# A two-layer decode kernel: the loads around the layers' border, in contiguous quarters into rooms that come free by quarters

## The chip, the cores and the metric

The kernel runs on one core of one Trainium2 chip. The metric is the time of one execution in microseconds on the device; where several runs are shown, their median counts.

## The reference, cut to what matters

Four sequences decode one token each through two layers that share their weights and caches. Each layer is attention, then a feed-forward block:

```
x = x + attention(layernorm(x), k_cache, v_cache, wq, wo)
x = x + ffn(layernorm(x), w_gate, w_up, w_down)        # both lines twice
q = x @ wq                                             # 32 heads of 128, 4 to each of 8 key heads
o = softmax(q k^T / sqrt(128)) v  over 8192 keys;      out = o @ wo
ffn = (silu(x @ w_gate) * (x @ w_up)) @ w_down         # 512 -> 1792 -> 512
```

All tensors are bf16. One pair of a sequence and a key head, called a unit here, has 2 MB of keys and 2 MB of values (2.097 million bytes each); there are 32 units in a layer. The order of the 8192 keys of a unit makes no difference to the result, as long as keys and values are laid out in the same order.

## The kernel before, in words

**Rooms.** SBUF has eight rooms (slots 0 to 7 of `kvf`, line 200) of 2 MB: 128 partitions by 8192 elements, each in eight places of 1024 elements (`s{slot}.{q}`). A room takes the keys (K) or the values (V) of one unit. Slots 6 and 7 also take the feed-forward weights at the end of a layer (lines 202 to 212): the gate's from the start of slot 6 to the end of its place 6, a quarter of up's over the border of both slots, then down's in slot 7, in parts of 6, 6 and 2 of its 14 row blocks (`WD`, line 213). The other three quarters of up's weights have a room of their own.

**Order of the loads.** SP issues all transfers on one queue, in the order of the list `items` (lines 321 to 327). `pump` (line 373) issues the next ones as long as the room that `home` names (line 336) is free, and stops at the first whose room isn't. SP waits at each transfer until those who used the places are done. A whole unit is one transfer with rows of 32 KB (`runs`, line 345), wherever the rows fall. The last V of a layer (`split`, line 328) comes in four quarters of the free dimension, with rows of 4 KB.

**The border.** The second layer visits the units in the order 29, 30, 31, 0, 1, 2 and so on (line 310), because K and V of units 29 to 31 stay in slots 0 to 5 from the first layer (`kept`, line 320) and aren't loaded again. Below, K0 means the keys of unit 0 in the second layer, and so on. After the feed-forward weights the list goes on with K0, K1, V0, K2, V1, K3, V2, K4, V3, K5, V4, K6. K0 and K1 go to slots 6 and 7 once the last matmul with the down weights is done (`ffn`, lines 731 and 732). V0 takes K29's room and K2 takes K30's in two halves each (`halves`, line 330, and `half`, line 405), with rows of 8 KB, as the scores of the fourth and of the last of eight blocks are done (lines 538 to 541). V1, K3, V2 and V3 take the rooms of V29, K31, V30 and V31, K4 and K5 those of K0 and K1, V4 that of V0, K6 that of K2.

**Order of the work.** For a K, VectorE turns each block by a transpose of 32 x 32 (`turn`, line 451), and TensorE makes scores of it (`scores`, line 469, four matmuls a block); K29 to K31 are turned already. `keys` (line 527) writes down turning and scores block by block, the turning up to three blocks ahead. Then follow the maximum, the exponentials on ScalarE, and the transpose of the probabilities (`max_p` to `total`, lines 480 to 513), in steps of a list `line` that are put between the blocks after it. `values` (line 551) makes the weighted sums. A layer's list of work (`work`, line 312) is K29, K30, V29, K31, V30, K0, V31, K1, V0, K2, V1 and so on. The query projection is made for the first unit's heads at the start of a layer and for all others in one block (`qproj`, line 676): in the second layer in front of K0's scores (lines 807 and 808). GpSimd places a unit's query for its scores (`place_q`, line 459). TensorE's, VectorE's and ScalarE's instructions are recorded first and then played, the regular units as a loop (`roll`, line 740). In the second layer the loops begin with K2. All of them are issued from the helper lines 99 and 117, and the transfers from lines 133 and 135; so the profile has tiles rather than lines to go by.

Of the kernel before, what the change touches and what calls it, by code (L numbers as in the profile page):

```python
# [145 lines left out]
def bass_interleave_layers__gqa_block_cached__swiglu_ffn__decode_kernel(  # L146
# [44 lines left out]
    with ExitStack() as es:  # L191
# [75 lines left out]
        sem_h = [[sem(f"sem_h{k}{i}") for i in range(2)] for k in range(2)]  # L267
# [105 lines left out]
        def pump():  # L373
            while issued[0] < len(items):
# [19 lines left out]
                src = cache[b, g, :, :].rearrange("(p t) d -> p (t d)", p=P)  # L394
# [10 lines left out]
        def half(it, i):  # L405
            to = halves[it]
            kind, L, u = to
            s = slot_of[it]
            if i == 0:
                assert items[issued[0]] == to  # L410
                slot_of[to] = s
                issued[0] += 1
            w = SL // 2
            src = (A_k_cache if kind == "K" else A_v_cache)[u % B, u // B, :, :].rearrange("(p t) d -> p (t d)", p=P)
            T.dma("sp", [(kv[:, s, i * w:(i + 1) * w], src[:, i * w:(i + 1) * w])], sem_h[unit_order[1].index(it[2])][i],
                  writes=[f"s{s}.{i * NB // 2 + k}" for k in range(NB // 2)])

        def finished(it):
            kind, L, u = it
            if (kind, 1, u) in kept and L == 0:  # L420
                slot_of[kind, 1, u] = slot_of[it]
                if kind == "K":
                    turned.update((1, u, q) for q in range(NB))
            elif it in halves:
                half(it, 1)
                pump()
            else:
                free.add(slot_of[it])
                pump()
# [97 lines left out]
        def keys(L, u):  # L527
            def block(q):
# [9 lines left out]
                if q == NB // 2 - 1 and ("K", L, u) in halves:  # L538
                    half(("K", L, u), 0)
# [4 lines left out]

            for q in range(NB):
                if (L, u, q) not in turned:
                    turn(L, u, q)
                blocks.append((0.65, lambda q=q: block(q)))
                drain(LAG)
        done = set()  # L550
        def values(L, u):
# [36 lines left out]
            def add_rows():  # L588
                T.pe(bank(LNB)[:, 0:REP], acc[:], head[:], reads=["acc", "head"], writes=[f"pb{LNB}"],
                     start=True, stop=True)  # L590
                scale_o(LNB)
# [16 lines left out]
            def scale_o(k):  # L608
                T.op("dve", lambda e: e.tensor_tensor(oT[:, g // (G - 1), :, b], bank(k)[:, 0:REP], rl[:, rl_of[u], :],
# [66 lines left out]
        def qproj(gs, u=None):  # L676
            h0, nh = gs[0] * REP, len(gs) * REP
            for h in range(h0, h0 + nh):
                for kt in range(KT):
                    T.pe(bank(LNB)[:, h * B:(h + 1) * B], wq_sb[:, kt, h * Dh:(h + 1) * Dh], xn[:, kt * B:(kt + 1) * B],  # L680
                         start=(kt == 0), stop=(kt == KT - 1),
                         reads=[f"wq{kt}", "xn"], writes=[f"pb{LNB}"], sig=(kt == KT - 1))
            T.op("dve", lambda e: e.tensor_copy(qT[:, :, h0:h0 + nh],
# [15 lines left out]
        def ffn(last):  # L699
# [4 lines left out]
            rb = rstd[:].unsqueeze(1).to_broadcast([P, FO, B])  # L704
            for (w_sb, wname, bk) in (([wg_sb[:, k, :] for k in range(KT)], "wg", gb), (wu_sb, "wu", ub)):
                for fo in range(FO):
# [16 lines left out]
            for j, (a, b) in enumerate(WD):  # L723
                for nt in range(KT):
                    for fo in range(a, b):
                        T.pe(bank(dn[j])[:, nt * B:(nt + 1) * B], wd_sb[:, fo, nt * P:(nt + 1) * P],
                             hT[:, fo * B:(fo + 1) * B], start=(fo == a), stop=(fo == b - 1),
                             reads=["hT", f"wd{j}"] + at_w["wd"], writes=[f"pb{dn[j]}"], sig=(fo == b - 1))
                if j < len(WD) - 1:
                    add_to_x(dn[j])  # L730
            free.update((NKEEP, NKEEP + 1))
            pump()
# [65 lines left out]
        for L in range(2):  # L798
# [4 lines left out]
            qproj([first], unit_order[L][0])  # L803
            rest_q = [list(range(0, first)), list(range(first + 1, G))]
            assert (L, first) in ((0, 0), (1, G - 1))
            for i, (kind, _, u) in enumerate(work(L)):
                if L == 1 and (kind, u) == ("K", 0):
                    blocks.append((3.5, lambda gs=rest_q[0]: qproj(gs)))
                (keys if kind == "K" else values)(L, u)
                if L == 0 and i == 0:  # L810
                    drain(0.0)
                    qproj(rest_q[1])
# [45 lines left out]
```

## Time and profile before

| what | value |
|---|---|
| median of 3 runs | 650.14 us (649.64 to 650.25) |
| the profiled execution's own time | 651.29 us |
| its span, from the first to the last instruction | 649.3 us |
| TensorE (matmul) busy | 505.3 us, 78% |
| VectorE busy | 446.2 us, 69% |
| ScalarE busy | 116.3 us, 18% |
| moved by the transfers | 274.27 MB, a mean of 422 GB/s |
| mean granted TensorE clock | 0.855 |

The busy share of an engine is an average over the whole span. The kernel has a start, the first layer, a border of some 60 us around 350 us, the second layer, and an end, with different limits. So the views by stretches of time are of more use than the sums, above all those of the transfers: the rate in GB/s and the times of SP's issues.

### The profile page before, as it was taken

How to read it: one execution, taken by the hardware profiler on the slowest of the kernel's cores; microseconds unless marked ns; L12 is line 12 of the kernel's file. 1: busy time of each engine (PE TensorE's matmuls, PEld its weight loads, DVE VectorE, ACT ScalarE, POOL GpSimd, SP SyncE). 2: the span in 40 equal slices, each digit the busy share in tenths (PEclk: the TensorE clock that was granted, in tenths of full speed). 3: DMA queues.
4: the chain of work that ended last, by engine and by line, in shares of the span. 5: the costliest groups of instructions: out<-in, count | busy, mean ns of one | idle time of the engine just before them, and what ended most of it. 6: DMA issues, size and time to landing. Idle time of an engine off the chain costs nothing.

```text
span 649.3 us, 12407 instructions
## 1 busy us (share of the span) xinstructions
PE 505.3 (78%) x4896; PEld 324.7 (50%) x4896; DVE 446.2 (69%) x1079; ACT 116.3 (18%) x391; POOL 19.3 (3%) x73
## 2 busy tenths in 40 slices
PE   1657788878868787886877986898888787886886
PEld 1534454545435454553556654555555454553556
DVE  2556676776866767776762386979797777686683
ACT  0021111211211212221220211213131221121120
POOL 0000000000000000000000000000000000000000
PEclk9998787797987879789795978979897969799795
DMA  8999999999999999999999999999999999999996
GB/s 347 427 431 428 433 429 434 428 440 428 432 436 424 444 426 432 439 424 442 428 416 361 421 408 430 417 439 430 432 438 424 438 430 436 436 424 438 430 415 279
DMA packets 13085, 274.27 MB, mean 422 GB/s; under 512 B 2712, under 2 KB 2720, under 8 KB 3744
## 3 DMA queue, kind: packets, MB, share of 16 engines
q1 hardware_dynamic: 13056, 273.89, 98.7%
q8 instruction: 17, 0.28, 0.2%
q14 instruction: 12, 0.10, 0.0%
HBM read 273.88 MB, written 0.00 MB: 422 GB/s over the span
## 4 chain that ended last, share of the span: by engine, by line
DMA 50%; DVE 24%; PE 21%; issue 3%; SPq 1%; ACT 1%; DVEq 0%; POOL 0%; ACTq 0%; POOLq 0%
DMA kvf<-in_A_k_cache_dram 47%; PE ps L99 21%; DVE kvf L117 15%; DVE acc L117 4%; DMA kvf<-in_B_w_up_dram 3%; DVE one L117 1%; DVE pT L117 1%; SPq L135 1%; DVE m L117 1%; DVE scr L117 1%; ACT pb L117 0%; ACT acc L117 0%; DVE oT L117 0%; DVEq L782 0%; SPq L133 0%
## 5 line engine op out<-in xcount | busy, mean ns | idle before, releaser
L117 DVE STREAM_TRANSPOSE kvf<-kvf 128x512 f32<-128x512 f32 x488 | 322.3, 686 | 68.6 <-DMA kvf<-in_A_k_cache_dram 68.6
L99 PE MATMUL ps<-kvf,zq 128*128 128x256 bf16 x2048 | 332.6, 305 | 21.7 <-DVE kvf L117 16.4
L99 PEld LDWEIGHTS ps<-kvf,zq 128*128 128x128 bf16 x2048 | 202.6, 111 | 92.7 <-DVE kvf L117 40.2
L117 ACT ACTIVATE pb<-m 1x128 f32<-1x128 f32 x64 | 19.7, 308 | 441.1 <-DVE m L117 441.1
L99 PE MATMUL ps<-kvf,pT 128*16 128x512 bf16 x960 | 68.0, 407 | 1.4 <-DVE rl L117 1.4
L117 DVE SCALAR_TENSOR_TENSOR acc<-ps,own,acc 128x128 f32<-128x128 f32 x180 | 63.2, 351 | 6.5 <-ACT acc L117 1.9
L99 PE MATMUL ps<-identf,one 128*1 128x128 f32 x64 | 17.9, 279 | 43.2 <-DVE one L117 43.2
L117 DVE TENSOR_REDUCE one<-ps 128x1 f32<-128x256 f32 x64 | 25.9, 405 | 37.0 <-PE ps L99 36.5
L99 PEld LDWEIGHTS ps<-identf,one 128*1 128x1 f32 x64 | 5.1, 80 | 73.6 <-DVE one L117 67.5
L99 PE MATMUL ps<-head,acc 128*128 128x4 f32 x120 | 24.5, 275 | 21.4 <-DVE acc L117 21.3
L99 PEld LDWEIGHTS ps<-head,acc 128*128 128x128 f32 x120 | 20.5, 214 | 37.0 <-DVE acc L117 36.7
L117 ACT ACTIVATE pb<-ps,one,rstd 128x256 bf16<-128x256 f32 x64 | 36.1, 563 | 2.1
L467 POOL TENSOR_TENSOR zq<-scr,quad 128x64 bf16<-128x64 bf16 x62 | 18.1, 293 | 604.0 <-PE ps L99 564.9
L99 PEld LDWEIGHTS ps<-kvf,pT 128*16 128x16 bf16 x960 | 19.1, 91 | 33.8 <-issue 21.9
L99 PE MATMUL ps<-one,pb 1*128 1x1 f32 x128 | 26.2, 272 | 11.5 <-ACT pb L117 11.2
L99 PEld LDWEIGHTS ps<-one,pb 1*128 1x128 f32 x128 | 20.8, 202 | 28.8 <-ACT pb L117 26.0
L99 PE MATMUL ps<-o,wo_sb 128*128 128x4 bf16 x256 | 26.5, 166 | 9.1 <-DVE o L117 9.1
L117 DVE STREAM_TRANSPOSE pT<-pb 128x256 bf16<-128x256 bf16 x64 | 26.1, 408 | 9.7 <-ACT pb L117 9.7
L99 PEld LDWEIGHTS ps<-rsm,one 128*128 128x128 f32 x128 | 23.9, 232 | 12.2 <-ACT rsm L117 10.4
L99 PEld LDWEIGHTS ps<-o,wo_sb 128*128 (+1 forms) x256 | 22.8, 103 | 12.8 <-issue 9.0
L99 PE MATMUL ps<-rsm,one 128*128 128x4 f32 x128 | 21.7, 240 | 9.0 <-ACT rsm L117 9.0
L117 DVE TENSOR_TENSOR xT<-xT,ps 128x16 f32<-128x16 f32 x21 | 3.6, 172 | 33.1 <-PE ps L99 33.1
(61 smaller groups left out, 197.1 us busy)
## 6 DMA issues: line engine op xcount, KB each, us to landing
kvf<-in_A_k_cache_dram SPq DMA_DIRECT2D x60, 2048.0 KB, 28.8
kvf<-in_A_v_cache_dram SPq DMA_DIRECT2D x58, 2048.0 KB, 31.2
wq_sb<-in_A_wq_dram SPq DMA_DIRECT2D x4, 1024.0 KB, 8.4
wo_sb<-in_A_wo_dram SPq DMA_DIRECT2D x8, 512.0 KB, 37.7
kvf<-in_A_v_cache_dram SPq DMA_DIRECT2D x8, 512.0 KB, 14.7
kvf<-in_B_w_gate_dram SPq DMA_DIRECT2D x8, 448.0 KB, 16.8
kvf<-in_B_w_down_dram SPq DMA_DIRECT2D x14, 256.0 KB, 17.6
kvf<-in_B_w_up_dram SPq DMA_DIRECT2D x5, 448.0 KB, 18.0
```

The source lines that it names most:

```text
L99: return e.matmul(out, lhsT=lhsT if at is None else lhsT(place(at)), rhs=rhs, **kw)
L117: self.tape[engname].append((repr((name, args, kw)), lambda e, _: getattr(e, name)(*args, **kw), left, sig, None))
L135: ins = e.add_instruction(mybir.InstDMACopy(name=self.nc.get_next_instruction_name(), mode="Copy", queue="qSPDynamicHW", ins=e.lower_ap_dm ...
L467: T.op(eng, lambda e: e.tensor_tensor(dst, q4, m4_, ALU.mult), reads=keys_ + ["quad"], writes=["zq"])
```

## The change

The feed-forward weights' rooms are given up in pieces: three quarters of K0 are issued once the gate's matmuls are written down, the fourth after up's, half of K1 after the first part of down's, the other half at its end. For that, down's parts become 8, 4 and 2 row blocks, and each part waits for its own places alone. The rooms of K29 and K30 are given up by quarters, after every second block, not by halves. Each of these pieces is a contiguous quarter of the cache (2048 keys, 512 KB, rows of 16 KB). Units 0, 1 and 2 of the second layer and the last unit of both layers are loaded in such quarters, keys and values alike (`fours`), so that both have the same order. V31's values come ahead of K0's scores and behind the query projection, which is now split into seven blocks of matmuls (`qmul`) and one step behind them (`qrows`). V3 stands ahead of K4 in the list of loads. The blocks of K0 are turned among the scores of K30, those of K1 among K31's (`ahead`). The list of VectorE's instructions shows these 16 transposes at their new places; the loops begin with K2 as before, and TensorE has the same matmuls. The sum over rows in `add_rows` gets columns of its own in its bank.

```diff
+        WD = ((0, 8), (8, 12), (12, 14))
-                "wd": room(f1, f1 + FO * D)}
-        WD = ((0, 6), (6, 12), (12, 14))
+                **{f"wd{j}": room(f1 + a * D, f1 + b * D) + [f"wd{j}"] for j, (a, b) in enumerate(WD)}}
...
+        i, j = (items.index((k, 1, unit_order[1][2 * NRES + n])) for k, n in (("K", 1), ("V", 0)))
+        items[i], items[j] = items[j], items[i]
...
-        halves = {("K", 1, unit_order[1][k]): items[ends[0] + 3 + k] for k in range(2)}
+        heirs = {("K", 1, unit_order[1][k]): items[ends[0] + 3 + k] for k in range(2)}
+        fours = {(L, unit_order[L][-1]) for L in range(2)} | {(1, u) for u in unit_order[1][NRES:2 * NRES]}
...
                 if it in split:
-                    w = TT * Dh // NQ
-                    n8 = NB // NQ
+                    n = NB // NQ
                     for q in range(NQ):
-                        T.dma("sp", [(kv[:, s, q * w:(q + 1) * w], src[:, q * w:(q + 1) * w])], sem_l[q],
-                              writes=[f"s{s}.{q * n8 + k}" for k in range(n8)])
+                        part(it, s, q * n, (q + 1) * n, sem_l[q])
+                elif (L, u) in fours:
+                    part(it, s, 0, NB, sem_s[s])
...
+        def part(it, s, a, b, sem_):
+            kind, L, u = it
+            assert (L, u) in fours
+            n = NB // NQ
+            w, m = n * TB * Dh, S // NQ
+            src = (A_k_cache if kind == "K" else A_v_cache)[u % B, u // B, :, :]
+            T.dma("sp", [(kv[:, s, q * w:(q + 1) * w], runs(src[q * m:(q + 1) * m, :])) for q in range(a // n, b // n)],
+                  sem_, writes=[f"s{s}.{k}" for k in range(a, b)])
...
+        def quarter(it, i):
+            to = heirs[it]
             if i == 0:
+                place(to, slot_of[it])
+            n = NB // NQ
+            part(to, slot_of[it], i * n, (i + 1) * n, sem_h[unit_order[1].index(it[2])][i])
...
-                if q == NB // 2 - 1 and ("K", L, u) in halves:
-                    half(("K", L, u), 0)
+                if ("K", L, u) in heirs and (q + 1) % (NB // NQ) == 0 and q < NB - 1:
+                    quarter(("K", L, u), q // (NB // NQ))
...
+            i = unit_order[L].index(u)
+            ahead = unit_order[1][i + 2] if L == 1 and i in (1, 2) else u
             for q in range(NB):
-                if (L, u, q) not in turned:
-                    turn(L, u, q)
+                if (L, ahead, q) not in turned:
+                    turn(L, ahead, q)
...
+                if not last:
+                    if bk == gb:
+                        place(ks[0], NKEEP)
+                        part(ks[0], NKEEP, 0, w6, sem_p[0])
+                    else:
+                        part(ks[0], NKEEP, w6, NB, sem_p[1])
...
+                if j == 0 and not last:
+                    place(ks[1], NKEEP + 1)
+                    part(ks[1], NKEEP + 1, 0, NB // 2, sem_p[2])
+            if not last:
+                part(ks[1], NKEEP + 1, NB // 2, NB, sem_p[3])
...
+            if L == 1:
+                todo.remove(("V", 1, unit_order[1][2]))
+                todo.insert(todo.index(("K", 1, 0)), ("V", 1, unit_order[1][2]))
+            for i, (kind, _, u) in enumerate(todo):
+                if L == 1 and (kind, u) == ("V", unit_order[1][2]):
+                    for k in rest_q[0]:
+                        blocks.append((0.5, lambda k=k: qmul([k])))
+                    blocks.append((0.5, lambda gs=rest_q[0]: qrows(gs)))
```

More of the change, by code (lines that the diff above doesn't have):

```diff
@@ L266, in bass_interleave_layers__gqa_block_cached__swiglu_ffn__decode_kernel @@
         sem_l = [sem(f"sem_l{q}") for q in range(NQ)]
-        sem_h = [[sem(f"sem_h{k}{i}") for i in range(2)] for k in range(2)]
+        sem_h = [[sem(f"sem_h{k}{i}") for i in range(NQ)] for k in range(2)]
+        sem_p = [sem(f"sem_p{i}") for i in range(4)]
         sem_x = sem("sem_x")
@@ L403, in pump, with place @@
                 issued[0] += 1
[L405 to L408, printed above, removed]
-            if i == 0:
[L410 to L416, printed above, removed]
+        def part(it, s, a, b, sem_):
[6 more added lines that the diff above has]
+                  sem_, writes=[f"s{s}.{k}" for k in range(a, b)])
+        def place(it, s):
+            assert items[issued[0]] == it
+            slot_of[it] = s
+            issued[0] += 1
+        def quarter(it, i):
+            to = heirs[it]
+            if i == 0:
+                place(to, slot_of[it])
+            n = NB // NQ
+            part(to, slot_of[it], i * n, (i + 1) * n, sem_h[unit_order[1].index(it[2])][i])
         def finished(it):
@@ L423, in finished @@
                     turned.update((1, u, q) for q in range(NB))
-            elif it in halves:
-                half(it, 1)
+            elif it in heirs:
+                quarter(it, NQ - 1)
                 pump()
@@ L674, in deviation, with qmul @@
                  reads=["vs", bkey], writes=["rstd"])
-        def qproj(gs, u=None):
-            h0, nh = gs[0] * REP, len(gs) * REP
-            for h in range(h0, h0 + nh):
+        def qmul(gs):
+            for h in range(gs[0] * REP, (gs[-1] + 1) * REP):
                 for kt in range(KT):
@@ L802, in bass_interleave_layers__gqa_block_cached__swiglu_ffn__decode_kernel @@
             first = unit_order[L][0] // B
[L803 removed]
+            qmul([first])
+            qrows([first], unit_order[L][0])
             rest_q = [list(range(0, first)), list(range(first + 1, G))]
             assert (L, first) in ((0, 0), (1, G - 1))
[L806 to L808 removed]
+            todo = work(L)
+            if L == 1:
[6 more added lines that the diff above has]
+                    blocks.append((0.5, lambda gs=rest_q[0]: qrows(gs)))
                 (keys if kind == "K" else values)(L, u)
```

20 lines of the change are left out of this document (11 added, 9 removed).

## The prediction, made before the change was run

> **What bounds the kernel now.** I read the page's queues and its chain of waits first.
>
> ```profile
> q1 hardware_dynamic: 13056, 273.89, 98.7%
> ...
> DMA 50%; DVE 24%; PE 21%; issue 3%; SPq 1%; ACT 1%; DVEq 0%; POOL 0%; ACTq 0%; POOLq 0%
> ```
>
> The reader is to see that the transfers fill 98.7% of the span of 16 DMA engines, and that no other engine carries more than a quarter of the chain. So time is saved only where the transfers pause. Next, busy time by stretches; the last number of a row is GB/s, the one before it the busy share of the DMA engines, the third from the end the TensorE clock.
>
> ```profile
> 50.00:300.00 250.00, 198.79 (x1601) 122.43 (x1599) 178.12 (x418) 44.76 (x152) 7.61 (x26) 0.83 1.00 432
> 300.00:346.00 46.00, 36.18 (x500) 25.47 (x501) 29.46 (x79) 8.91 (x31) 0.88 (x3) 0.84 1.00 423
> 346.00:354.00 8.00, 4.74 (x111) 4.03 (x108) 2.05 (x12) 0.00 (x0) 0.00 (x0) 0.50 0.84 301
> 354.00:384.00 30.00, 27.68 (x316) 19.69 (x320) 12.58 (x33) 5.63 (x19) 1.17 (x4) 0.81 1.00 427
> 384.00:388.00 4.00, 3.35 (x35) 2.11 (x28) 3.92 (x10) 1.77 (x6) 0.00 (x0) 1.00 0.85 295
> ```
>
> The steady rate is 432 GB/s. Against it, 300 to 354 us loses 46 x (1 - 423/432) + 8 x (1 - 301/432) = 1.0 + 2.4 = 3.4 us, 354 to 384 loses 0.35, and 384 to 388 loses 4 x (1 - 295/432) = 1.3. Those 5.0 us are the ceiling of any gain at the border. Who feeds the queue there stands in the timeline of SP's issues (start, duration, count):
>
> ```profile
> 326.77 9.42 SPq L135 DMA_DIRECT2D kvf<-in_B_w_down_dram  x7
> 347.99 2.38 SPq L135 DMA_DIRECT2D kvf<-in_A_k_cache_dram  x2
> 356.84 3.07 SPq L133 DMA_DIRECT2D kvf<-in_A_v_cache_dram  x2
> 362.13 2.85 SPq L133 DMA_DIRECT2D kvf<-in_A_k_cache_dram  x2
> 365.63 0.48 SPq L135 DMA_DIRECT2D kvf<-in_A_v_cache_dram  x1
> 370.70 0.48 SPq L135 DMA_DIRECT2D kvf<-in_A_k_cache_dram  x1
> 371.69 0.47 SPq L135 DMA_DIRECT2D kvf<-in_A_v_cache_dram  x1
> 383.63 0.47 SPq L135 DMA_DIRECT2D kvf<-in_A_k_cache_dram  x1
> ...
> 390.67 0.47 SPq L135 DMA_DIRECT2D kvf<-in_A_k_cache_dram  x1
> ...
> 403.00 0.47 SPq L135 DMA_DIRECT2D kvf<-in_A_k_cache_dram  x1
> ```
>
> SP has nothing to issue from 336.2 to 347.99, and from 372.2 to 383.63: each time the queue runs dry behind it. The two transfers issued into the dry queue (347.99 and 383.63) show what that costs, in the issues by line with size and time to landing:
>
> ```profile
> kvf<-in_A_k_cache_dram SPq DMA_DIRECT2D x1, 2048.0 KB, 8.0
> kvf<-in_A_k_cache_dram SPq DMA_DIRECT2D x1, 2048.0 KB, 8.3
> ```
>
> A unit of 2.097 MB moves in 4.85 us at 432 GB/s, so an issue must come some 3.3 us before the queue is empty. My rule below: a transfer lands at the later of (the one ahead of it; its issue + 3.3), plus 4.85 us per unit or 1.21 per quarter. Tried on before, it gives K0 356.1, K1 361.0, V0 365.7, K2 370.6, V1 375.4, K3 380.3, V2 385.1, K4 383.63 + 3.3 + 4.85 = 391.8, and then V3 396.6, K5 401.5, V4 406.3.
>
> **Part 1, K0 and K1 in the feed-forward weights' rooms.** TensorE's timeline:
>
> ```profile
> 342.87 0.89 PE L99 MATMUL ps<-xn,kvf 128*128 128x4 bf16 x28
> 344.74 1.50 PE L99 MATMUL ps<-xn,kvf 128*128 128x4 bf16 x51 [0.98 <-DMA kvf<-in_B_w_up_dram]
> 347.62 0.29 PE L99 MATMUL ps<-xn,kvf 128*128 128x4 bf16 x5 [1.38 <-issue]
> 348.22 1.65 PE L99 MATMUL ps<-scr,kvf 128*128 128x4 bf16 x56 [0.31 <-DVE scr L117]
> ...
> 354.04 5.45 PE L99 MATMUL ps<-kvf,zq 128*128 128x256 bf16 x28
> ...
> 361.00 1.05 PE L99 MATMUL ps<-kvf,zq 128*128 128x256 bf16 x8
> ...
> 364.50 1.04 PE L99 MATMUL ps<-kvf,pT 128*16 128x512 bf16 x16
> ...
> 371.63 2.94 PE L99 MATMUL ps<-xn,wq_sb 128*128 128x4 bf16 x112
> ...
> 376.47 1.03 PE L99 MATMUL ps<-kvf,zq 128*128 128x256 bf16 x4 [0.83 <-POOL zq L467]
> ...
> 379.96 3.60 PE L99 MATMUL ps<-kvf,zq 128*128 128x256 bf16 x20
> ```
>
> The gate's matmuls end at 343.8, so three quarters of K0 are issued there; its last at 347.9 (up ends), K1's first half at 349.3 (32 of the 56 down matmuls), its second at 349.9. SP stands idle then and is not late; a quarter's issue takes it 0.33 to 0.5 us, as its rows show. Weights are issued by 336.2, ahead in the same queue, so they are not held up. With the weights landed by about 349.0, the rule gives K0 353.9 and K1 358.7: the queue does not run dry. The waits added at SP hold only transfers behind them that could not start earlier anyway.
>
> **Part 2, V0 and K2 by quarters.** K29's scores run from 352.9 to 359.5, 0.68 us per block (half way falls at the issue of 356.84), so V0's quarters are issued at 355.4, 356.8, 358.2 and 359.6 and land at 360.0, 361.3, 362.7, 364.1. K30's give K2's at 361.1, 362.1, 363.4, 364.65: landings 365.7, 366.9, 368.1, 369.3. V1 (V29's room, 365.6) lands at 374.1, K3 379.1, V2 383.9. Here the releases bind, and of the 2.4 us only 385.1 - 383.9 = 1.2 us is left.
>
> **Part 3, V31 ahead of K0, V3 ahead of K4.** V31's values move to just behind the query projection; V3 is issued at about 377.4, not behind K4. Needed by 383.9 - 3.3 = 380.6, it is in time: V3 lands at 388.8 where K4 landed at 391.8. The second pause (1.8 us by the rule) is gone; together 3.0 us at this point. K4 (K0's end, at the latest 384) is needed by 385.5, K5 by 390.3.
>
> **Part 4, K0 and K1 turned early.** VectorE's timeline:
>
> ```profile
> 359.54 0.42 DVE L117 TENSOR_REDUCE one<-ps 128x1 f32<-128x256 f32 x1 [6.53 <-PE ps L99]
> ...
> 376.99 2.48 DVE L117 STREAM_TRANSPOSE kvf<-kvf 128x512 f32<-128x512 f32 x4
> ```
>
> The same 16 transposes of 0.62 us go to where VectorE idled (6.5 us before K29's maximum). The first three stand ahead of that maximum in VectorE's order and wait for K0's landing: 353.9 + 1.9 = 355.8, before 359.5, so they hold nobody. Four more stand ahead of the transpose of K29's probabilities and delay it by up to 0.6 us, K30's by up to 0.5; V29 at 364.50 covers the first. Without cover: 0.5 us.
>
> What it buys is the compute chain that releases K6's room, and this decides how much of the 3.0 us stays. ScalarE's timeline:
>
> ```profile
> 46.95 0.26 ACT L117 ACTIVATE one<-ps,rstd 128x1 f32<-128x1 f32 x1 [6.47 <-issue]
> ...
> 398.42 0.26 ACT L117 ACTIVATE one<-ps,rstd 128x1 f32<-128x1 f32 x1 [5.40 <-issue]
> ```
>
> On entering its loop, in both layers, ScalarE stands for 5 to 6 us with nothing to wait for, and K2's last scores wait for its sums: hence K6 only at 403.0. After the change V4 lands at 403.3, so K6 must be issued by 400.0. The projection split in seven ends at about 375.5, V31 at 377.4, K0 starts then (376.5 before). Its 32 matmuls cost 0.18 us each (379.96's row, at half clock) or 0.13 (361.00's row). K0 ends at 384.0 if slow throughout, 382 if fast; K1, no longer bound by transposes, 4.9 later, at 388.9 or 387, against 390.6 (the issue at 390.67). The loop entry follows it: K6 at 401.2 or 399.3. Slow, the queue starves 401.2 + 3.3 - 403.3 = 1.2 us; fast, not at all. I take 0.5 (below), since both stretches of scores that began slow ended fast, after more than half of their time:
>
> ```profile
> 352.90:359.50 6.60, 6.57 (x34) 4.54 (x34) 0.11 (x1) 0.56 (x2) 0.00 (x0) 0.57 0.99 425
> 360.00:364.60 4.60, 4.60 (x41) 3.52 (x45) 0.91 (x3) 1.52 (x5) 0.00 (x0) 1.00 1.00 413
> 376.40:383.50 7.10, 6.79 (x40) 4.64 (x43) 5.87 (x13) 0.53 (x3) 0.01 (x1) 0.57 0.99 422
> ```
>
> The mean of 0.57 over 6.6 and 7.1 us is some 6 us at 0.5 and 1 us at 1.0; K0 follows V31, which starts the work at 376.4, so the last quarter of K0 should run fast: two thirds of the way from fast to slow, K6 at 400.5, 0.5 us. The Trainium skill (TensorE: Matmul & The Clock Gate, Part 1) states otherwise: some 3.4 us of sustained work double the clock. By that rule K0 would be fast from about 379.8, and the estimate would be no starving and -3.1 us in all; K29, busy 6.57 of 6.60 us at a mean of 0.57, speaks against it, and the trace goes into my sum.
>
> **Part 5, contiguous quarters.** In long runs:
>
> ```profile
> 330.00:332.50 2.50, 2.50 (x28) 1.76 (x31) 1.90 (x5) 1.21 (x4) 0.00 (x0) 1.00 1.00 411
> 361.00:369.00 8.00, 7.62 (x72) 5.27 (x70) 3.17 (x10) 3.29 (x11) 0.29 (x1) 1.00 1.01 421
> ```
>
> Rows of 4 KB go at 411, of 8 KB at 421, of 32 KB at 432; rows of 16 KB I put between the last two. V28 at the end gains 5.1 - 4.9 = 0.2 us, K28, now in four, loses 0 to 0.13. Net -0.1, between -0.2 and +0.1; those at the border lie in parts 1 to 3.
>
> **Sum.** -3.0 + 0.5 - 0.1 = **-2.6 us**. The profiled execution took 651.29 us, 2.0 more than its span of 649.3, and becomes 648.7; the median of the runs shown, 650.14, is 1.15 lower: **647.5 us**. 0.2% is 1.3 us, about what a measurement of this kernel can tell from no change.
>
> **Rivals.**
> - *Full clock.* K29's scores at K30's pace end at 357.6, not 359.5. K1 at 358.7 then hides V0's quarters; K2 lands at 368.4 instead of 369.3, compute is 2 us ahead and K6 never starves: -3.9 - 0.1, 646.1 us. For it: K30 ran at 1.00. Against: 0.57 over K29, after the same feed-forward.
> - *Taken back at ScalarE's loop entry.* K0 slow throughout and a stand of 6.47 us, as in the first layer: K6 at 402.3, 2.3 us of starving; -0.7 - 0.1, 649.3 us.
> - *Slower.* TensorE's unexplained stand of 1.38 us at 347.62 sits between gate and K29; the queue was draining then, now it is full. If it is the loading of code and takes ScalarE's 6.47 us, K29 and every release behind it come 5.1 us later: K6 is ready at 403.8 + 5.1 = 408.9 against 406.3 before, 652.6 us. It decides from a stand of about 5.3 us on (1.38 + 2.6 + 1.3). Against: the stand began while the engines were still almost full. The Trainium skill (Runtime: NRT & Kernel Launch, Instruction fetch mechanics) says that taken branches force a fetch, while straight code is prefetched; the trace agrees in that both long stands are loop entries.
> - *No effect.* Early transfers do start, but compute paces K6 as before, at 403.0: 650.1 us. Against: the transposes that filled VectorE from 377 to 382 are gone.
>
> **Chances.** Forecast 0.58 (646.6 to 648.8); full clock 0.15; taken back 0.14; slower 0.06; no effect 0.07. So faster 0.75, counting 0.02 of taken back, same 0.19, slower 0.06. The range 645.7 to 649.6 takes in the clock's bounds and taken back, and leaves out the two last and the tails.
>
> **What would show it.** First K issue at about 344; 346 to 354 above 415 GB/s; issues of V0's and K2's quarters as in part 2 with small dips there; V3 issued near 377 and no dip at 384; transposes between 352 and 371; K6 between 399.3 and 401.2, with a dip near 404 as long as it is late. It is wrong if K29 starts more than 1 us from 352.9, or if ScalarE's stand is not near 5.4 us.

## The result and the profile after

The changed kernel takes **649.48 us** (median of 20 runs, 648.33 to 650.64) against 650.25 us (20 runs, 649.10 to 652.38); the ratio is 0.9982, 95% interval 0.9976 to 0.9988. The kernel was measured beside the one before four more times (ratios 0.9966, 0.9977, 0.9969 and 0.9975), and once more as v_late (below, 0.9977). The mean of the six is 0.9974, or **1.7 us less**. The forecast was 2.6 us less. The sign and the range were right. The size was too large by half against the mean of the six, and more than twice too large against the first comparison (0.8 us by the medians, 1.2 by the ratio).

The profiled execution of the changed kernel took 648.33 us with a span of 646.4; it is the fastest of the 20, while that of the kernel before was 1.0 us slower than its median. So the two traces differ by 2.96 us, of which only part is the change. The queue and the chain, from the page after:

```profile
q1 hardware_dynamic: 12768, 273.90, 98.9%
...
DMA 54%; DVE 22%; PE 17%; SPq 3%; issue 3%; ACT 1%; DVEq 0%; POOL 0%; ACTq 0%; POOLq 0%
```

The transfers still set the time (98.9% of the span, 98.7% before). The stretches that were shown of before, from the windows of the changed kernel:

```profile
50.00:300.00 250.00, 195.13 (x1579) 120.27 (x1579) 178.19 (x418) 44.90 (x153) 7.33 (x25) 0.85 1.00 432
300.00:346.00 46.00, 36.80 (x505) 26.57 (x504) 28.54 (x76) 8.81 (x30) 0.88 (x3) 0.76 1.00 427
346.00:354.00 8.00, 4.95 (x103) 4.09 (x103) 3.23 (x14) 0.03 (x1) 0.00 (x0) 0.50 1.02 423
354.00:384.00 30.00, 27.65 (x330) 19.97 (x329) 16.91 (x42) 5.97 (x20) 1.17 (x4) 0.86 1.00 413
384.00:388.00 4.00, 4.00 (x42) 2.82 (x44) 1.88 (x6) 1.52 (x5) 0.24 (x1) 1.00 1.03 442
```

The reader is to see in the last column that both holes are closed (346 to 354 from 301 to 423 GB/s, 384 to 388 from 295 to 442), that the steady rate is the same, and that 354 to 384 has become slower, 413 instead of 427. SP's issues in the changed kernel:

```profile
342.23 8.52 SPq L135 DMA_DIRECT2D kvf<-in_A_k_cache_dram  x8
354.89 3.87 SPq L135 DMA_DIRECT2D kvf<-in_A_v_cache_dram  x4
359.57 3.99 SPq L135 DMA_DIRECT2D kvf<-in_A_k_cache_dram  x4
364.08 2.39 SPq L135 DMA_DIRECT2D kvf<-in_A_v_cache_dram  x4
...
370.47 8.05 SPq L135 DMA_DIRECT2D kvf<-in_A_v_cache_dram  x5
382.61 5.54 SPq L135 DMA_DIRECT2D kvf<-in_A_k_cache_dram  x2
...
399.50 0.47 SPq L135 DMA_DIRECT2D kvf<-in_A_k_cache_dram  x1
```

K0 and K1 are issued from 342.23 on, V0 and K2 in four pieces each, V3 as the last of the five at 370.47 (its issue ends at 378.5), K4 and K5 from 382.61, and K6 at 399.50 instead of 403.00. TensorE, ScalarE and VectorE, from the timelines of the changed kernel:

```profile
352.68 1.04 PE L99 MATMUL ps<-kvf,zq 128*128 128x256 bf16 x4 [0.41 <-DVE zq L117]
...
353.80 4.15 PE L99 MATMUL ps<-kvf,zq 128*128 128x256 bf16 x28
```

```profile
395.07 0.26 ACT L117 ACTIVATE one<-ps,rstd 128x1 f32<-128x1 f32 x1 [5.03 <-issue]
```

```profile
352.83 1.90 DVE L117 STREAM_TRANSPOSE kvf<-kvf 128x512 f32<-128x512 f32 x3
```

K29's scores start where they did (352.68, 352.93 before) but 28 of their matmuls take 4.15 us, not 5.45. ScalarE's stand at its loop entry is 5.03 us, and the turning of K0 has moved to 352.83.

### The profile page after: what moved, and what is told of

It is laid out like the page before. It is cut to its first block, busy times and chain, and to the rows that moved or that the text cites. A ratio compares the mean times of both kernels' runs of the same rounds, so it can differ in the third digit from the quotient of the medians.

```text
span 646.4 us, 12440 instructions
## 1 busy us (share of the span) xinstructions
PE 504.3 (78%) x4896; PEld 325.2 (50%) x4896; DVE 446.5 (69%) x1079; ACT 116.5 (18%) x391; POOL 19.3 (3%) x73
## 3 DMA queue, kind: packets, MB, share of 16 engines
q1 hardware_dynamic: 12768, 273.90, 98.9%
## 4 chain that ended last, share of the span: by engine, by line
DMA 54%; DVE 22%; PE 17%; SPq 3%; issue 3%; ACT 1%; DVEq 0%; POOL 0%; ACTq 0%; POOLq 0%
DMA kvf<-in_A_k_cache_dram 49%; PE ps L99 17%; DVE kvf L117 14%; DVE acc L117 4%; SPq L135 3%; DMA kvf<-in_B_w_gate_dram 3%; DMA kvf<-in_B_w_down_dram 2%; DVE pT L117 1%; DVE one L117 1%; DVE m L117 1%; DVE scr L117 0%; DVEq L808 0%; DVE oT L117 0%; ACT pb L117 0%; DVE o L117 0%
```

## The experiments

After the result there were three theories of the missing microsecond: A, the border gains what the two traces show and the first comparison was a low draw; B, a part is given back at the end or the start; C, the border itself varies from execution to execution with the clock, and the forecast was sized from a costly one. Each comparison of times is with the kernel before on the same chip. The loss of a stretch is worked out as in the prediction, its length times (1 - rate / 432). It is good to some 0.3 us, since packets count where they start: some stretches come out faster than the steady rate, by up to 0.3 us. The expectations of r_before and r_after were written before these names were given: their theory A is C here.

**Repeats: how much of the difference is the execution?** Seven runs are the two kernels unchanged.

r_before: 

> The kernel before once more, for a second trace. In the first trace the transfers lost 5.1 us against 432 GB/s between 320 and 412 us, and that execution took 1.0 us longer than the median. Theory A (the border's loss varies from run to run with the compute that releases the rooms): this trace has another loss there, 3.5 to 4.5 us if its time is near the median. Theory B (the border is the same each time, the start and the end vary): again 4.9 to 5.3 us, and the difference between runs lies before 20 us or behind the last V's landing. Timed: ratio 1.000 within its interval.

r_after: 

> The changed kernel once more. In its first trace, 1.15 us below its median, the loss from 320 to 412 us was 2.8 us, K29's scores ran mostly at full clock and ended at 358.0. Theory A: in a run near the median K29's or K0's scores run at half clock, the releases come later and the loss is 3.5 to 4.5 us. Theory B: 2.6 to 3.0 us again, and the time is lost at the end: more than 14 us from the last V's landing to the end of the span, where before had 13.6. Timed: ratio to before 0.9975 to 0.999.

r_after2: 

> The changed kernel once more, unchanged. Theory A (the border gains what the trace shows, and always): the transfers' loss around the border is again 2.6 to 2.8 us against 5.1 to 5.9 in the kernel before, and the time lies 2.2 us below the kernel before, as in the second comparison. Theory B (a part of it is given back elsewhere, by an amount that varies with the execution): the loss is again 2.6 to 2.8, but the time lies only 1.2 us below, as in the first comparison, and the missing microsecond stands at the end, behind the last landing (14.2 us and more, against 13.6), or at the start. Theory C (the border itself varies from run to run, with the clock at which K29 to K31 are worked off): the loss at the border is well above 2.8 in this trace.

r_after3: 

> The changed kernel, unchanged, as the standard for the three others. All theories: 1.2 to 2.2 us below the kernel before; by theory C the trace's loss at the border goes with the clock: 2.6 to 2.8 us if it rises within 3.3 us of K29's first score, 3.5 to 4 us if it takes over 5 us.

r_before2: 

> The kernel before, unchanged, for its trace. If the traced executions so far were costly ones, the transfers' loss around the border is 4.0 to 5.0 us here, with an earlier rise of the clock in K29 (under 5 us after its first score), against 5.1 and 5.9; if they were typical, it is 5 to 6 us again and the execution lies near 651 us.

r_before3: 

> The same once more, with the same two expectations: 4.0 to 5.0 us of loss around the border if the traces so far were costly executions, 5 to 6 us if they were typical.

r_after4: 

> The changed kernel, unchanged, beside v_tail2: 1.2 to 2.2 us below the kernel before, a loss of 2.6 to 3.6 us around the border, and 14.0 to 14.3 us behind V28's landing by the theory of the end, 13.4 to 14.3 if that stretch varies by itself.

An eighth was meant to undo the early issue, by moving K0's and K1's lines behind the down matmuls:

```diff
-                if not last:
-                    if bk == gb:
-                        place(ks[0], NKEEP)
-                        part(ks[0], NKEEP, 0, w6, sem_p[0])
...
+                place(ks[0], NKEEP)
+                part(ks[0], NKEEP, 0, w6, sem_p[0])
...
```

v_late: 

> The changed kernel with K0 and K1 issued together behind the last down matmul, as before the change, still in contiguous quarters. If the early issue is what closes the pause at 346 to 352 (both theories), the pause is back: a loss of 2.5 to 3 us there. What it is worth in time: 1.2 us if releases behind it bind anyway (V1 and K6 were bound by compute in my sum), 2.5 us or more if the transfers bind. Ratio to before then 0.9995 to 1.001 in the first case and 1.001 to 1.003 in the second.

It undoes nothing: a transfer waits for the last reader of its places, wherever its line stands, so SP has the same instructions and waits (K0's first issue at 342.31). Its ratio, 0.9977 (0.9966 to 0.9988), is one more of the changed kernel. Of the others, r_before has 1.0003 (0.9993 to 1.0012), r_after 0.9966 (0.9953 to 0.9978), r_after2 0.9977 (0.9967 to 0.9986), r_after3 0.9969 (0.9956 to 0.9982), r_after4 0.9975 (0.9964 to 0.9986); r_before2 and r_before3 are single executions. The traced execution of r_before (652.28 us, 6.0 us lost between 320 and 412 us) lies above both of its expectations; that of r_after repeats the first one. What the traces show, by kernel, in us:

| execution | own time | clock rises after K29's first score | loss 346 to 370 | 370 to 394 | 394 to 420 | K6 landed |
|---|---|---|---|---|---|---|
| before, profiled | 651.29 | 5.70 | 2.7 | 1.3 | 0.2 | 412.69 |
| r_before | 652.28 | 5.42 | 3.6 | 1.3 | -0.2 | 412.81 |
| r_before2 | 650.45 | 3.54 | 2.8 | 0.3 | 0.5 | 410.80 |
| r_before3 | 650.08 | 3.98 | 2.2 | 0.5 | 0.5 | 411.58 |
| after, profiled | 648.33 | 2.96 | 1.6 | -0.3 | 0.7 | 409.07 |
| r_after | 648.53 | 3.19 | 1.5 | -0.2 | 0.2 | 409.38 |
| r_after2 | 649.68 | 5.14 | 2.1 | -0.2 | 0.6 | 410.05 |
| r_after3 | 649.12 | 5.37 | 1.5 | 0.1 | 1.1 | 409.84 |
| r_after4 | 650.16 | 5.19 | 2.3 | -0.1 | 0.9 | 410.74 |
| v_late | 651.05 | 5.75 | 2.9 | -0.1 | 1.2 | 412.87 |

Two things are to be seen. In each kernel the executions in which the clock rises early (under 4 us after K29's first score) are the quick ones. And at a like rise the change is worth less than between the two profiled executions: K6 lands on average 1.9 us earlier among the late risers, 2.0 among the early ones, 1.6 over all, against 3.6 between the profiled pair. So theory A falls, and C fits both the spread and the size, as far as ten traces go.

Why the rise varies stands in windows cut at the changes of the clock. The kernel before (profiled execution), then the changed kernel:

```profile
338.15:358.63 20.48, 14.57 (x278) 12.05 (x275) 4.70 (x25) 1.37 (x5) 0.00 (x0) 0.50 0.92 368
358.63:375.70 17.07, 15.77 (x247) 11.59 (x244) 5.64 (x17) 3.87 (x14) 0.58 (x2) 1.00 1.02 429
375.70:382.53 6.83, 5.82 (x29) 3.97 (x30) 6.54 (x15) 1.20 (x4) 0.29 (x1) 0.50 1.06 453
```

```profile
335.16:355.64 20.48, 13.75 (x318) 11.91 (x318) 6.84 (x30) 1.37 (x5) 0.00 (x0) 0.50 1.01 420
355.64:372.71 17.07, 15.92 (x208) 11.70 (x206) 12.86 (x31) 4.79 (x17) 0.59 (x2) 1.00 1.00 401
372.71:379.54 6.83, 6.13 (x86) 3.95 (x84) 2.65 (x8) 0.64 (x2) 0.29 (x1) 0.50 0.96 410
```

The stretches at half and at full clock are all multiples of 3.41 us (20.48, 17.07, 6.83) in both kernels: the clock changes on a grid whose place is another in each execution, here by 3.0 us. K29 starts at the same time but meets the grid elsewhere. In the ten traces the rise comes with the end of the first step that K29's scores fill but for some 0.5 us at most: in the four with an early rise the first score falls at most 0.45 us behind the start of a step, or up to 0.6 us ahead of one; in the six others it falls 1.1 to 1.7 us behind the start of a step, and the rise waits for the next. Since K0's rise is seven steps behind K29's (23.9 us in all ten), an execution that draws a late rise has it twice. K4 of the kernel before, whose room K0's scores release, is issued at 383.2 and 383.6 then, and at 381.8 and 382.0 with an early rise. For the second hole of the kernel before, r_before2 with its early rise, in windows and in SP's issues:

```profile
354.00:370.00 16.00, 15.12 (x136) 10.57 (x134) 4.80 (x14) 3.77 (x13) 0.58 (x2) 0.93 0.97 394
370.00:394.00 24.00, 20.99 (x271) 14.38 (x263) 19.39 (x45) 4.10 (x14) 0.88 (x3) 0.86 1.00 426
```

```profile
381.82 0.47 SPq L135 DMA_DIRECT2D kvf<-in_A_k_cache_dram  x1
```

K4 is issued at 381.82, 1.8 us earlier than in the profiled execution (383.63), and the hole at 384 is all but gone without any change: 24 x (1 - 426 / 432) = 0.3 us instead of 1.3. The same stretch in the profiled execution, in r_before and in r_before3, and then the first hole in r_before, r_before2 and r_before3 (301 GB/s in the profiled execution):

```profile
370.00:394.00 24.00, 21.28 (x275) 14.10 (x273) 18.10 (x43) 4.10 (x14) 0.88 (x3) 0.86 0.98 409
370.00:394.00 24.00, 21.05 (x274) 14.00 (x272) 18.47 (x43) 4.10 (x14) 0.88 (x3) 0.86 0.98 408
370.00:394.00 24.00, 21.20 (x271) 14.44 (x263) 19.18 (x45) 4.10 (x14) 0.88 (x3) 0.86 1.00 423
```

```profile
346.00:354.00 8.00, 4.80 (x103) 4.03 (x103) 2.04 (x12) 0.03 (x1) 0.00 (x0) 0.50 0.99 375
346.00:354.00 8.00, 5.13 (x103) 4.27 (x104) 2.05 (x12) 0.09 (x1) 0.00 (x0) 0.50 0.94 355
346.00:354.00 8.00, 5.18 (x113) 4.34 (x111) 2.05 (x12) 0.20 (x1) 0.00 (x0) 0.50 1.00 387
```

**The early issue, undone by a wait.** The lines are moved as in v_late, and SP waits for all readers of both rooms before K0's first quarter; v_four2 also has V31 and V3 at their old places and no early turning.

```diff
+                T.wait_res("sp", writes=places)
                 place(ks[0], NKEEP)
                 part(ks[0], NKEEP, 0, w6, sem_p[0])
```

v_late2: 

> The changed kernel, but SP waits for the last matmul of the feed-forward before it issues the first quarter of K0, some 349.5 to 350 instead of 342.3. By the prediction (2.4 us of pause at 348 to 354, of which the releases behind it leave half): the pause of 1.5 to 2.9 us is back before K0's first landing, which comes at 356 to 357, K1 lands at 361 to 362, V0 and K2 then hide behind K1 and lose 0.5 or less instead of 1.4 to 2.1, and the time is 1 to 1.3 us above the changed kernel (ratio to the kernel before 0.9990 to 0.9995). If the early issue only moves the loss from K0 to V0 and K2, whose rooms are released by the scores all the same: within 0.4 us of the changed kernel (0.9970 to 0.9980).

v_four2: 

> Contiguous quarters and the release by quarters alone: K0 issued behind the feed-forward, V31 and V3 at their old places, no early turning. With the early issue, v_four was at 0.9994. If the early issue is worth 1 us or more by itself, this one is slower than the kernel before (1.0005 to 1.002). If it only moves the loss, 0.9990 to 1.0000.

v_late2 has 1.0029 (1.0019 to 1.0040), v_four2 1.0024 (1.0014 to 1.0035): both slower than the kernel before. Windows and SP's issues of v_late2:

```profile
346.00:354.00 8.00, 5.03 (x111) 4.24 (x108) 2.04 (x12) 0.11 (x1) 0.00 (x0) 0.50 0.53 193
354.00:370.00 16.00, 14.85 (x119) 10.57 (x118) 12.62 (x27) 3.74 (x13) 0.58 (x2) 0.89 1.01 407
```

```profile
349.61 5.29 SPq L135 DMA_DIRECT2D kvf<-in_A_k_cache_dram  x8
355.00 4.58 SPq L135 DMA_DIRECT2D kvf<-in_A_v_cache_dram  x4
```

The hole of 346 to 354 costs 8 x (1 - 193 / 432) = 4.4 us, and V0 and K2, now behind a late K1, lose 0.9 instead of 1.4 to 2.9. Without the early issue the changed kernel takes 3.6 us more: 1.0029 against a mean of 0.9974. This undoes more than the change did, though: before, K0 was issued as soon as up's matmuls were done (346.25 to 347.99 in four traces), not behind down's, as the description of the kernel before has it; here it is issued behind down's at 349.61. How much of the 3.6 us is the change's own is therefore not shown: v_four2, held back in the same way, is 1.6 us slower than the kernel before, although it keeps a part of the change. Both expectations of v_late2 miss: the loss moves for about 1 us of it (0.9 at V0 and K2 where the changed kernel loses 1.9 on average), and the rest is dearer than the 1 to 1.3 us of the first. Of v_four2's two, the first holds.

**V31 and V3, and the parts beside the early issue.** In v_noswap V31 stands behind K0's scores and V3 behind K4 again. v_four leaves the early turning out as well.

```diff
-        i, j = (items.index((k, 1, unit_order[1][2 * NRES + n])) for k, n in (("K", 1), ("V", 0)))
-        items[i], items[j] = items[j], items[i]
...
-            if L == 1:
-                todo.remove(("V", 1, unit_order[1][2]))
-                todo.insert(todo.index(("K", 1, 0)), ("V", 1, unit_order[1][2]))
...
-                if L == 1 and (kind, u) == ("V", unit_order[1][2]):
+                if L == 1 and (kind, u) == ("K", 0):
```

v_noswap: 

> V31's values behind K0's scores and V3 behind K4 again, the rest of the change kept. By the prediction's rule K4 is then issued at K0's end, about 380.5 to 382, and is needed 3.3 us before V2 has landed (384.6): by 381.3. Theory 1 (the order of V31 and V3 takes the pause away): K4 is late, a dip of 0.5 to 1.2 us comes back between 384 and 388, and the time is 0.4 to 1 us above the changed kernel. Theory 2 (turning early took it away already, since K0 ends in time once its scores no longer wait for transposes): no dip at 384, and the time is the changed kernel's within 0.3 us.

v_four: 

> Of the change only the contiguous quarters and the release of K29's and K30's rooms by quarters are left: K0 and K1 are issued behind the last matmul of the feed-forward, V31 and V3 stand at their old places, K0 and K1 are turned at their scores. If the parts add up as the prediction has them, 1.2 of 5.0 us would be lost less at V0 and K2 at the most, the pauses at 348 and 384 are back, and the time lies 0 to 0.6 us below the kernel before. If early issue and early turning are two ways to the same gain (each alone missing cost 0.7 us), both missing costs 1.4 to 2.2 and the time equals that of the kernel before, or is slower by up to 0.3 because of the smaller pieces.

Since moving the lines changed no wait, v_four still has the early issue (K0's first at 342.37), which its expectation took away. v_noswap has 1.0012 (1.0003 to 1.0021), v_four 0.9994 (0.9986 to 1.0003), r_after2 beside them 0.9977. The stretch of the second hole in v_noswap, with SP's issue of K4, and then in v_four:

```profile
370.00:394.00 24.00, 21.25 (x268) 14.89 (x259) 9.89 (x27) 4.10 (x14) 0.88 (x3) 0.79 0.92 377
```

```profile
384.09 0.47 SPq L135 DMA_DIRECT2D kvf<-in_A_k_cache_dram  x1
```

```profile
370.00:394.00 24.00, 20.67 (x274) 14.30 (x263) 19.10 (x43) 4.10 (x14) 0.88 (x3) 0.86 0.98 408
```

Theory 1 holds, and by more than it said: with the transfers ahead moved up and K4 not issued before 384.09, the hole is 3.1 us wide (1.3 in v_four), and the time 2.3 us above the changed kernel (0.0035 of 650.65). A part of the 3.1 us is the clock of this one execution, in which K0's 32 score matmuls take 6.51 us, all at half clock (5.24 in v_four's). Early issue without the new order gives its gain back at the next empty queue: v_noswap is slower than the kernel before, and v_four can't be told from it.

**The early turning.** v_noahead turns K0 and K1 at their own scores again.

```diff
-            ahead = unit_order[1][i + 2] if L == 1 and i in (1, 2) else u
+            ahead = u
```

v_noahead: 

> The changed kernel without turning K0 and K1 early: each K is turned among its own scores. If the compute chain up to K6's release binds (my part 4), K1 ends near 390 instead of 387.7, K6 is issued 2 to 3 us later than the 399.5 of the changed kernel, the queue runs dry near 404 and the time goes up by 1.5 to 2.5 us. If the transfers bind, nothing changes within 0.5 us.

It has 0.9977 (0.9967 to 0.9987), with r_after at 0.9966 beside it: the intervals overlap. Its K6 is issued at 401.94 after a rise of 6.12 us, where the changed kernel's late risers have 400.94 to 402.73. So the 1.5 to 2.5 us of the first expectation are not there. What the turning is worth stays open; against the mean of the six it is not over some 1 us.

**The end.** v_tail loads the last unit of the second layer as before.

```diff
-        fours = {(L, unit_order[L][-1]) for L in range(2)} | {(1, u) for u in unit_order[1][NRES:2 * NRES]}
+        fours = {(0, unit_order[0][-1])} | {(1, u) for u in unit_order[1][NRES:2 * NRES]}
...
```

v_tail: 

> Only the last unit of the second layer is loaded as before (K28 in one transfer, V28 in strided quarters with rows of 4 KB), the rest of the change kept. Theory B (the end gives back a part of the border's gain, because the contiguous quarters let the last block of values come later in the work): the stretch behind V28's landing falls from 14.1-14.2 us to 13.6, and the time is 0.5 us below the changed kernel. By the prediction (contiguous quarters gain 0.1 at the end): V28 lands 0.1 to 0.2 us later with the same stretch behind it, and the time is 0.1 us above the changed kernel, which is not to be told from no change.

v_tail2: 

> The changed kernel with the last unit of the second layer loaded as before, once more. If the end gives back a part of the gain: 0.4 to 0.6 us below r_after4, and 13.4 us or less behind V28's landing against 14.0 to 14.3. If v_tail's distance was chance: within 0.2 us of r_after4.

v_tail has 0.9970 (0.9961 to 0.9980) beside 0.9977, v_tail2 0.9978 (0.9968 to 0.9989) beside 0.9975. The two differ in sign, so the 0.45 us of the first can't be told from chance, and nothing is left for the theory that the end gives a part back. From V28's landing to the end of the span it is 13.7 to 14.3 us in the five traces of the changed kernel that carry its name, 13.5 to 14.6 in the four of before, 13.4 and 13.6 in v_tail and v_tail2.

**A busy TensorE ahead of K29.** If the clock's grid is what varies, work that computes nothing might start the rise in time. 33 matmuls of 128 columns fill TensorE's waits between the gate's matmuls and K29's scores, in the changed kernel (a_warm), in that of v_tail (t_warm) and in the kernel before (b_warm).

```diff
+        def warm(n):
+            for k in range(n):
+                T.pe(bank(STEP)[:, 0:P], wq_sb[:, 0, 0:P], wq_sb[:, 0, 0:P], start=True, stop=True,
+                     reads=["wq0"], writes=[f"pb{STEP}"], sig=(k == n - 1))
...
+                    warm(14 if bk == gb else 2)
...
+                    warm((1, 4, 4)[j])
```

a_warm: 

> The changed kernel with 33 matmuls of 128 columns that compute nothing used, put where TensorE waits between the gate's matmuls and K29's scores. In ten traces so far the clock rose from half to full between 2.9 and 6.1 us after K29's first score, and K6 was issued at 399.4 to 399.5 where it rose early and at 401.3 to 401.7 where it rose late. Theory C (this is what makes the border's gain vary, and the forecast took the late rise of one execution as the rule): with TensorE busy through the waits the clock rises before or soon after K29's first score in each execution, V0's last quarter is issued by 357.5, K6 by 399.5, the loss around the border is 2.6 us or less and the time is 0.3 to 1 us below the unchanged r_after3 of the same call. Rival (the rise hangs on K29's own matmuls, or the spread of the times comes from elsewhere): the rise stays between 2.9 and 6.1 us, and the time is the same or up to 0.3 us more.

b_warm: 

> The kernel before with the same matmuls at the same places. Theory C: the rise comes early here too, V0's halves are issued some 1.5 us earlier (355.3 instead of 356.8), a part of the pause stays because K0 is issued behind the feed-forward as before; the time is 0.5 to 1.2 us below the kernel before, and the distance from a_warm is 1.2 to 2 us. Rival: no change of the time within 0.3 us, or up to 0.5 us more, since the matmuls stand in the chain ahead of K0's issue.

t_warm: 

> The changed kernel with the last unit of the second layer loaded as before (as in v_tail) and with the added matmuls (as in a_warm). If both effects are real and independent, the time lies below the kernel before by the sum: 1.8 for the change, 0.4 to 0.5 for the end, 0.3 to 1 for the clock, so 2.5 to 3.2 us. If v_tail's 0.45 us was chance, it equals a_warm within 0.3 us.

Theory C's forecast of the times fails: a_warm 1.0007 (0.9992 to 1.0021), t_warm 0.9993 (0.9981 to 1.0005), b_warm 1.0002 (0.9992 to 1.0012), with r_after3 at 0.9969 beside them, and a_warm's runs spread over 5 us (648.45 to 653.70). The trace of a_warm, in windows and then TensorE's timeline:

```profile
335.35:355.83 20.48, 17.57 (x354) 14.76 (x354) 6.98 (x31) 1.37 (x5) 0.00 (x0) 0.50 1.01 421
...
354.00:370.00 16.00, 14.85 (x132) 10.55 (x134) 12.21 (x28) 3.85 (x13) 0.58 (x2) 0.94 1.00 399
...
394.00:420.00 26.00, 21.93 (x181) 14.00 (x182) 19.99 (x47) 6.47 (x22) 0.88 (x3) 0.88 0.96 399
```

```profile
395.50 1.88 PE L99 MATMUL ps<-kvf,zq 128*128 128x256 bf16 x8 [6.57 <-issue]
```

TensorE, busy 17.57 of the 20.48 us, stays at half clock all the same, also through the step of the grid ahead of K29 (349.01 to 352.42), of which it is busy for 3.27 us; the rise comes 3.09 us after K29's first score (2.54 in t_warm, 2.25 in b_warm), a little early but still inside K29. V0 and K2 do lose a little less (1.2 us in a_warm, 1.0 in t_warm, against 1.4 in the two early draws without the added matmuls; 0.2 between 354 and 370 in b_warm). What costs time in their traces is something else: with the longer program TensorE itself stands for 6.57 us as it enters its loop (5.86 in t_warm), where the unchanged kernel has 0.2, K6 is issued at 402.14, and 394 to 420 loses 2.0 us. b_warm has no such stand (0.26 us), but its earlier transfers lose 1.9 us between 370 and 394, where v_noswap's lose 3.1. So this experiment doesn't separate the clock from the rest by its times; it is a second change in itself.

## Why the prediction was right in direction and wrong in size

- **The step that failed is part 3:** "The second pause (1.8 us by the rule) is gone". It is gone (-0.1 us on average between 370 and 394), and v_noswap shows that the new order is what removes it. But it is not 1.8 us wide to begin with: 0.9 us on average in four traces of the kernel before, 1.3 in the two with a late rise, 0.3 and 0.5 in the others. The forecast read K4's issue at 383.63 from one execution and took it for the kernel's; it goes with the clock's draw. The rule then made 1.8 of it where the row itself said 1.3. The trace showed that the rule was off: V2 landed at 387.10 in it, not at the rule's 385.1, and K4 was issued 3.5 us before that, not into a dry queue. Of the 1.2 us by which -3.0 was too much, 0.8 lies in this term (1.0 instead of 1.8) and 0.4 in parts 1 and 2.
- **Parts 1 and 2** were to bring 1.2 us. Between 346 and 370 the loss falls from 2.8 to 2.0 us, 0.8. The first hole, too, was read from one execution: 346 to 354 loses 2.4 us in it, but 0.8 to 1.4 in the three others of the kernel before, where TensorE stands for at most 0.74 us at that place instead of 1.38 and K0 is issued at 346.25 to 346.52. V0 and K2 then lose 1.4 to 2.5 us behind it, instead of 0.3. Part 1 by itself is right: 346 to 354 loses 0.1 to 0.2 us after the change, and in the profiled execution K0 and K1 land at 354.0 and 358.9, forecast 353.9 and 358.7. So is its reason that the loss passes on to V0 and K2. These land at 364.1 and 369.0 (364.1 and 369.3), although their quarters were issued up to 1.6 us earlier than forecast: a quarter needed more than the 3.3 us of the rule. The first, issued 4.03 us before K1's landing, still landed 0.35 us later than a full stream would have it (360.48 against 358.92 + 1.21).
- **Part 4** has the right number: 394 to 420 loses 0.5 us more than before, the 0.5 that the forecast gave for the starving at K6. A part of that is luck, for it mixes 0.9 among the late rises with -0.1 among the early ones. K6's issue was forecast to move from 403.0 to 400.5; on average it moved from 402.0 to 401.0, since 403.0 again was one execution's (401.6 to 401.8 in the three others). By the forecast's own figures K0 ends at 377.4 + 32 x 0.18 = 383.2 or 377.4 + 32 x 0.13 = 381.6, not at 384.0 or 382. ScalarE's stand was 4.85 to 5.86 us in the six traces, as taken; that the turning bought anything is not shown.
- **Part 5:** the net of -0.1 us is not told from nothing (v_tail and v_tail2).
- **The sum** by the traces' means is thus -0.8 - 1.0 + 0.5 = -1.3 us, -1.6 by K6's landing, and -1.7 by the times, not -2.6. The excess of the profiled execution over its median, 1.15 us, was carried over as a constant. Most of it sat in the very stretches that the change touches: against r_before2 and r_before3 that execution took 0.8 and 1.2 us longer and lost 0.6 and 1.0 us more between 346 and 420. So it had to be taken off the gain.
- **Full clock**, the rival: half right. A rise early in K29 is what some executions draw (four of ten), and K6 hardly starves then: 394 to 420 loses 0.7 and 0.2 us, and 0.5 in both early traces of the kernel before. But there is less to gain, since the early draw narrows the holes of the kernel before as well (0.3 and 0.5 us at 384): by the own times the change is worth 1.8 us among the early rises, not 4. The argument against it, K29 busy for 6.57 of 6.60 us at a mean of 0.57, was one draw of the grid. The Trainium skill (TensorE: Matmul & The Clock Gate, Part 1) says not only 3.4 us but that the window is free-running, "it doesn't reset when your kernel starts". The traces agree, with steps of 3.41 us and a rise 3.0 to 5.8 us after the first score; the ±500 ns that it gives for the variation is too little for these 2.8 us. The prediction used half of that rule.
- **Slower**, by a code-loading stand ahead of K29: did not happen; K29's first score comes between 351.6 and 353.2 in the ten traces. A stand of that size came with a longer program at another place, in a_warm and t_warm; that it is the loading of code is not shown.
- **Taken back** would be a ratio of 0.9987, which lies above each of the six, though inside the intervals of two; **no effect** is excluded by their intervals and by the closed holes.

Not settled: the worth of the early turning alone and of the early issue as the change made it, why the first of the six comparisons gives less than the five others, and what decides whether TensorE stands at its loop entry. The spread of the times is tied to the rise of the clock by ten traces, not by an experiment that sets the rise.

## What to carry to other kernels

A hole in the queue of transfers that hangs on a compute chain has another width in each execution; size it from several traces, and where the profiled execution lies above the median, suspect that the excess is in the hole and take it off the gain. Closing one hole passes the loss on to the next place where the queue runs empty, so an early issue pays only together with an order that keeps the queue fed behind it (v_noswap 1.0012 without that order, 0.9977 with it). Before an experiment undoes a step by moving a line, make sure that the wait moves with it.

## What the runs showed of the hardware that was not expected

- TensorE's clock changes on a grid of 3.41 us that starts anywhere: stretches of 6.83, 17.07 and 20.48 us in both kernels, with the rise 3.0 to 5.8 us after the first of the scores that bring it.
- Matmuls of at most 128 columns that kept TensorE recorded as busy ahead of K29, for 3.27 us of a step of 3.41 in a_warm (349.01 to 352.42), did not raise the clock; in the changed kernel's profiled execution a step with 3.00 busy us (352.23 to 355.64), most of them K29's scores of 256 columns, did. So the recorded busy time alone does not tell whether the clock rises.
- With 33 more matmuls in straight code far ahead, TensorE stood for 6.57 us (a_warm) and 5.86 us (t_warm) at its loop entry, where it had been 0.2 us; in b_warm it did not (0.26 us). The runs of a_warm spread over 5 us.
- Eight quarters issued into an empty queue from 349.61 on took 14.1 us to the last landing (363.74), where two whole transfers, issued from 347.99 on while the weights were landing (349.00), took 14.0 (361.98): no saving by the pieces is to be seen once the queue is dry.
